# Linear attention and MLP block on one core: the last w2 chunk's raw rows loaded earlier, its split and its repeated rows moved later, the packed squares moved earlier

## The chip, the cores and the metric

The kernel runs on one core of one Trainium2 chip. The metric is the time of one execution on the device in microseconds (us); lower is better. Five engines work side by side, each through its own instructions in their written order: TensorE (PE, with its weight loads PEld), VectorE (DVE), ScalarE (ACT), GpSimd (POOL) and SyncE (SP), which here issues nearly all DMA transfers.

## The reference

```
x  : (2048, 512)          xn = layernorm(x)
A  : q, k, v = xn @ wqkv  (32 heads of 16)
     pq, pk = phi(q), phi(k);  phi(t) = (t + 1 if t > 0 else exp(t)) + 1e-6
     kv = sum over tokens of pk * v;  z = sum over tokens of pk
     o  = (pq @ kv) / (pq . z + 1e-6);   A = o @ wo
B  : h = xn @ w1 + b1     (F = 1376)
     B = relu(h)^2 @ w2 + b2
out = x + A + B
```

## The kernel before

All matrix work is in fp32 precision, made of fp32r matmuls: each operand is split into a high half (a ScalarE copy that rounds, `copy("act", h, t)`) and a low half (a VectorE subtraction, `rest_of`), and a product takes three passes: high x high, high x low, low x high (`three`, `product`).

The first part (to about 98 us in the profile) walks over 16 tiles of 128 tokens: layer norm, transpose, k projection, and the products `kx` of tokens with pk, whose column sums are also the key sum z. After it ScalarE copies the four banks of `kx` (`kxs`) and one row (`zrow`), and SyncE moves that row to DRAM (`zd`, line 878) and back as columns (`zc`, line 882, four transfers).

The second part does two rounds (n = 0, 1) of two 512-token blocks, t1 and t2. A round is a loop over passes p; each pass takes one pair of chunks of q or of w1 (`order`: q0, w0, q1, w1, ...) through a Strassen-like scheme of seven half-size products in four PSUM banks. The order of the work is written out by hand, with `manual_schedule`, so every engine runs its instructions as the lines stand. In a pass:

- A = `A11` x x1, copied by ScalarE to c11; B = `A12` x x1; VectorE adds them.
- C = `S1` x `T[1]`, copied by ScalarE to t5 (the page calls the tile t). In passes after the first, the bank `before` of the last pass is read by VectorE (line 1066) at the pass's start, and `A22` x `T[4]` is added into it after S1.
- In pass 0 of round 0, `last_sums(3, ...)` splits the token differences T[3], and `matrix()` multiplies the value sums with wo into four banks pm, which `matrix_copy(0..3)` copies to m.
- The next pass's chunk is split (`chunk_split`, tiles aop) and summed (`chunk_sums`, tiles S).
- A = `S2` x `T[2]`, copied by ScalarE to c12 (the page calls the tile c); then `S4` x x2 is added into C; VectorE adds C and c12 (line 1175). `last_sums(4, ...)` splits T[4].
- A = `S3` x `T[3]`, into the bank that c12 was copied from.

Hidden units go into the output through w2. w2 chunks are loaded raw (`piece_2`) and split into `w2r`; the closures that split wait in `w2next` and are run by `next_2` and `high_2`. The last chunk (f = NF - 1) has only 96 rows, 64 + 32. It is loaded in three pieces (line 207). Its `high()` rounds it, sends 64 rows by DMA to the low tile (line 211), and sends 32 rows four times to `w2q` (line 215); its `low()` does two VectorE subtractions. The hidden units of that chunk are packed the same way: `last_units` squares them (line 961), copies them to `sz` and sends 64 rows by DMA (`hidden_last`, line 465); `sz_rests` and `packed` subtract later. `last_2` uses sz and the last w2 chunk in pass 1, in the PSUM banks that pm had; `quarters_2` uses w2q after the loop.

Raw rows, w1 and q chunks and the sums S share six buffers ("raw"); a new one is loaded when an older one has had its last reader. wvl, a row of wqkv that is subtracted from wv in the first part (line 683), is one of them.

Of the kernel before, what the change touches and what calls it, by code (L numbers as in the profile page):

```python
# [8 lines left out]
F32R = mybir.dt.float32r  # L9
# [9 lines left out]
def kernel(  # L19
# [40 lines left out]
    NF = -(-F // P)  # L60
# [11 lines left out]
    keep = ctx.enter_context(tc.tile_pool(name="keep", bufs=1))  # L72
# [5 lines left out]
    def bank(name, tag="ps"):  # L78
        return psum.tile([P, 512], F32, name=name, tag=tag)

    def w512(name, tag, bufs):
        return work.tile([P, 512], F32, name=name, tag=tag, bufs=bufs)
# [8 lines left out]
    def two(name):  # L91
        return keep.tile([P, 2, 512], F32, name=name, tag=next_tag("x"))

    def four(name, tag, dt=F32, pool=None):
        return (pool or work).tile([P, TB, 512], dt, name=name, tag=tag)
# [4 lines left out]
    def f32(ap):  # L100
        return ap.bitcast(F32)
# [7 lines left out]
    def copy(eng, o, i, bias=0.0):  # L109
        if eng == "act":  # L110
            nc.scalar.activation(o, i, AF.Copy, bias=bias)  # L111
        elif bias:
            ENG[eng].tensor_scalar(o, i, bias, None, op0=OP.add)
        else:
            ENG[eng].tensor_copy(o, i)
# [5 lines left out]
    def rest_of(l, src, h):  # L121
        nc.vector.tensor_tensor(out=l, in0=src, in1=f32(h), op=OP.subtract)  # L122
# [40 lines left out]
    def raw(name, src):  # L163
        t = w512(name, "raw", 6)
        nc.sync.dma_start(t[:, :src.shape[-1]], src)
        return t
# [6 lines left out]
    def units(f):  # L173


        if f < NF - 1:
            return [(0, f * P, P)]
        return [(0, f * P + Q, 2 * Q), (2 * Q, f * P, Q), (3 * Q, f * P, Q)]
# [5 lines left out]
            nc.sync.dma_start(tj[:, :, a:a + n], w1[:, o:o + n].rearrange("(j p) n -> p j n", j=NJ))  # L184
        return t

    w2r = []

    def load_o():
        o = wos[0] = four("wo", "ra")  # L190
# [6 lines left out]
    def piece_2(f, at):  # L197

        h, l = w2s[f] = [w2r[at // 2][:, at % 2 * 2 + u] for u in range(2)]
        if f < NF - 1:  # L200
            t = raw(f"r2_{f}", w2[f * P:(f + 1) * P, :])
            return [lambda: copy("act", h, t), lambda: rest_of(l, t, h)]


        t = w512(f"r2_{f}", "raw", 6)
        for a, o, n in units(f):
            nc.sync.dma_start(t[a:a + n], w2[o:o + n, :])

        def high():
            copy("act", h, t)  # L210
            nc.sync.dma_start(f32(l[2 * Q:]), f32(h[:2 * Q]))
            if "q" not in w2s:
                w2s["q"] = work.tile([P, D], F32R, name="w2q", tag="w2q")
                for k in range(TB):
                    nc.sync.dma_start(f32(w2s["q"][k * Q:(k + 1) * Q]), f32(h[2 * Q:3 * Q]))

        def low():
            rest_of(l[:2 * Q], t[:2 * Q], h[:2 * Q])
            rest_of(h[3 * Q:], t[3 * Q:], h[3 * Q:])

        return [high, low]
# [230 lines left out]
    def quarters(name, r, h, pool, tag):  # L452

        lq = pool.tile([P, P], F32R, name=f"{name}q", tag=tag)
        for k in range(TB):
            at, to = slice(2 * Q, 3 * Q), slice(k * P, (k + 1) * P)
            rest_of(lq[k * Q:(k + 1) * Q], r[at, to], h[at, to])
        return lq

    def hidden_last(name, r):  # L460

        s = pair(name)
        h, hl = s[:, 0], s[:, 1]
        copy("act", h, r)
        nc.sync.dma_start(f32(hl[:2 * Q]), f32(h[:2 * Q]))

        def rests():
            rest_of(hl[2 * Q:], r[:2 * Q], h[:2 * Q])

        return (h, hl), rests  # L470

    def relu(o, i, f):
        nc.scalar.activation(o, i, AF.Relu, bias=b1s[:, f:f + 1])

    def plain_1(ps, w, x):

        for j in range(NJ):
            three(ps, [w[:, u, j * P:(j + 1) * P] for u in range(2)],
                  [x[u][:, j, :] for u in range(2)], j == 0, j == NJ - 1)
# [63 lines left out]
    for i0 in range(0, NT, TB):  # L543
# [5 lines left out]
        n = TB if i0 >= NPE else TB // 2  # L549
# [105 lines left out]
    def tokens_sum(n, tag):  # L655
        return keep.tile([P, 2, 2, 512], F32R, name=f"T{n}", tag=tag)
# [51 lines left out]
    def load_1(kind, n):  # L708
        load = raw_1 if kind == "w" else raw_q
        return [load(2 * n + k).rearrange("p (c n) -> p c n", c=2) for k in range(2)]  # L710
# [25 lines left out]
    def do(what, k=1):  # L736
        for _ in range(k):
            if what:
                what.pop(0)()
# [41 lines left out]
    def more(i=None):  # L781

        if i is None or i > 12:
            do(extra, counts[0].pop(0))
# [77 lines left out]
        more(i)  # L862

    T.update({n: tokens_sum(n, f"A{n - 3}") for n in (3, 4)})
    xlast = [xsb[(b + 1) % 2] for b in (NB - 1, NB - 2)]
    more()
    pz = bank("pz0")
# [47 lines left out]
    def matrix_copy(j, ps):  # L915
        if j % 2 == 0:
            mraw.append(two(f"m{j}"))
        copy("act", mraw[j // 2][:, j % 2], ps[j])
# [5 lines left out]


    last = TB - 1
    w2r = [four(f"w2r{k}", f"C{k}", F32R, keep) for k in range(2)]
    for n in range(2):
        t1, t2 = NB - 1 - 2 * n, NB - 2 - 2 * n
        x1, x2 = xsb  # L930
# [29 lines left out]
        def last_units(rz):  # L960
            nc.scalar.activation(rz, rz, AF.Square)
            sz, rests = hidden_last(f"sz{n}", rz)

            def packed():
                lqs.append(quarters(f"sz{n}", rz, sz[0], work, "heads"))

            return sz, rests, packed
# [3 lines left out]
        if n == 0:  # L971

            more()
            pz2 = bank("pz0b")
            plain_1(pz2, z, x2)
            more()

            rz = r2[1]
            relu(rz, pz, NF - 1)
            relu(r2[NF - 1], pz2, NF - 1)  # L980
            do(extra, 2)
            values()
            do(extra, len(extra))
            w2next = piece_2(NF - 1, 0)
        else:
            w2next = []
            pz = bank(f"pz{n}", "acc")
            plain_1(pz, z, x1)
# [4 lines left out]
        if n:  # L993
            rz = w512(f"rz{n}", "p", 6)
            relu(rz, pz, NF - 1)
            sz, sz_rests, packed = last_units(rz)
# [5 lines left out]
        def next_2(t):  # L1002

            do(w2next, 2 - highs.pop(0))
            if t + 1 < NF and (n == 0 or t >= TB - 1):
                f = w2order[t + 1]
                w2next.extend(piece_2(f, place(f)))

        def high_2():
            do(w2next)  # L1010
            highs[0] = 1
# [36 lines left out]
        def step(k=1):  # L1048

            for _ in range(k):  # L1050
                do(steps[t1] or steps[t2])

        for p in range(NO + 1):
            at_p = AT[p]
            kind, k = order[p] if p < NO else ("", 0)
            fa, fb = 2 * k, 2 * k + 1

            was, k = order[p - 1] if p else ("", 0)
            pa, pb = 2 * k, 2 * k + 1
            A, before, B, C = banks[p % 2], banks[(p + 1) % 2], *banks[2:]  # L1060
# [17 lines left out]
            if kind:  # L1078
                c11 = w512(f"c11_{n}_{p}", "p", 6)
                copy("act", c11, A)  # L1080
                if n == 0 and p == 0:
                    next_2(0)
                product(B, A12, [x[:, 2:] for x in x1], True, True)
                if kind == "w":
                    high_2()
                nc.vector.tensor_tensor(out=c11 if kind == "w" else q[t1][:, fa], in0=B, in1=c11, op=OP.add)
                if kind == "w":
                    relu(c11, c11, fa)
                else:
                    steps[t1] += steps_of(t1, fa, parts=True)  # L1090
                step(at_p[0])
# [25 lines left out]
            if p == 0:  # L1117
                def last_sums(k, *what):
                    for f in what:
                        for j in range(2):  # L1120
                            f(k, j, o34[k - 3][:, j])

                last_sums(3, difference_high, difference_low)
            if p == 1:
                nc.vector.tensor_scalar(zc[:, 1], zc[:, 0], 1e-6, None, op0=OP.mult)
                acc = [bank(f"acc{t1}_{k}", "acc") for k in range(TB)]
# [6 lines left out]
            elif not was:  # L1133

                if n == 0:
                    pm = matrix()
# [17 lines left out]
                s12, s34 = chunk_sums(p + 1, w)  # L1154
            if p + 2 < NO:
                w = load_1(*order[p + 2])
            step(at_p[3])
            if p == NO - 1 and n:
                do(bias, 2)
# [10 lines left out]
                chunk_split(0, 1, s12)  # L1170
            step(at_p[4])
            if n == 0 and p == 0:
                matrix_copy(2, pm)
            product(C, S4, [x[:, 2:] for x in x2], False, True)
            nc.vector.tensor_tensor(out=c12 if kind == "w" else q[t2][:, fa], in0=C, in1=c12, op=OP.add)
            if kind == "w":
# [21 lines left out]
                second_sums()  # L1198
            step(at_p[6])
            if n == 0 and p == 0:  # L1200
                matrix_copy(3, pm)
                sz, sz_rests, packed = last_units(rz)
            product(A, S3, [T[3][:, u] for u in range(2)])
            if p == NO - 3 + 1 - n:
                load_res(t1)
# [26 lines left out]
        f = NF - 2  # L1232
# [36 lines left out]
        for e, f in enumerate(waiting[:-2]):  # L1269
# [14 lines left out]
            if n == 0 and 1 <= e < 5:  # L1284
                k, u = divmod(e - 1, 2)
# [68 lines left out]
```

## Time and profile before

| | |
|---|---|
| median of 3 runs | 413.15 us (412.41 to 414.46) |
| profiled execution | 413.63 us, span 411.9 us |
| PE busy | 404.0 us, 98% of the span |
| DVE, ACT, POOL busy | 302.2, 263.1, 49.7 us |
| DMA | 56.34 MB, mean 137 GB/s |
| chain that ended last | PE 89%, DMA 3%, ACT 2%, DVE 2% |

Times in a profile are microseconds from the span's start. A row of the timeline gives start, length, engine, line, operation, tile written <- tiles read, shapes and the number of merged instructions; in brackets stands the engine's idle time before it and what released it. A line is often a helper's: L111 is ScalarE's copy, L119 and L122 the subtraction that makes a low half, L130 and L485 the three-pass products, so the tile names tell the places apart. The ends of matmuls are modelled.

### The profile page before, as it was taken

The page shows a single profiled execution, that of the slowest core. Times are in us where ns is not written, and L with a number is a line of the kernel's source. Part 1 is how long each engine was busy: PE and PEld are TensorE (multiplying, and loading weights), DVE is VectorE, ACT ScalarE, POOL GpSimd, SP SyncE. Part 2 cuts the span into 40 slices and gives each one's busy share as a digit, 9 for nine tenths or more (in the row PEclk, how much of TensorE's full clock was granted, in tenths as well). Part 3 has the DMA queues.
Part 4 walks back from the last instruction along what each step waited for, and adds up shares of the span by engine and source line. Part 5 has one row for each costly group of instructions (what it writes and reads, how often), then busy time and mean ns, then how long its engine had stood idle before and what let it go on. Part 6 is the DMA issues. An engine that isn't in the chain of part 4 may idle for free.

```text
span 411.9 us, 5624 instructions
## 1 busy us (share of the span) xinstructions
PE 404.0 (98%) x1947; PEld 331.2 (80%) x1947; DVE 302.2 (73%) x550; ACT 263.1 (64%) x460; POOL 49.7 (12%) x83
## 2 busy tenths in 40 slices
PE   7999999999989999999999999999999999999996
PEld 6788888888678888888878888888888888878885
DVE  5885666587699898988449967567989686449833
ACT  4666667556687779788638631577587857737520
POOL 5442333220000000030000200000000200000200
PEclk9999999999999999999999999999999999999999
DMA  6949676800442221273357992411121881024612
GB/s 207 347 142 340 193 306 205 256 1 0 104 134 72 78 75 54 77 203 53 136 221 246 362 235 90 128 53 51 51 78 29 235 183 40 2 101 154 103 26 102
DMA packets 46462, 56.34 MB, mean 137 GB/s; under 512 B 8225, under 2 KB 29985, under 8 KB 45154
## 3 DMA queue, kind: packets, MB, share of 16 engines
q1 hardware_dynamic: 44130, 51.80, 38.9%
q0 software_dynamic: 2304, 4.20, 6.2%
q8 instruction: 15, 0.25, 0.2%
q14 instruction: 13, 0.11, 0.1%
HBM read 41.43 MB, written 13.37 MB: 133 GB/s over the span
## 4 chain that ended last, share of the span: by engine, by line
PE 89%; DMA 3%; ACT 2%; DVE 2%; issue 1%; SPq 1%; POOL 0%; ACTq 0%
PE acc L130 37%; PE b L485 29%; PE kx L386 10%; PE pk L366 9%; PE acc L496 2%; DMA x<-in_A_x_dram 1%; PE pz L130 1%; DMA r<-in_B_w_dram 1%; PE b L130 1%; DMA sz<-sz 1%; ACT T L111 0%; SPq L522 0%; ACT aop L111 0%; ACT kxs L111 0%; DVE aop L119 0%
## 5 line engine op out<-in xcount | busy, mean ns | idle before, releaser
L130 PE MATMUL acc<-w2r,s 128*128 128x512 f32 x477 | 112.8, 390 | 0.0
L130 PEld LDWEIGHTS acc<-w2r,s 128*128 128x128 f32 x477 | 89.4, 188 | 19.2 <-issue 0.7
L485 PE MATMUL b<-T,aop 128*128 128x512 f32 x336 | 83.6, 390 | 1.4 <-ACT c L111 1.4
L485 PEld LDWEIGHTS b<-T,aop 128*128 128x128 f32 x336 | 62.9, 188 | 15.6 <-ACT c L111 1.8
L1034 POOL DMA_DIRECT2D res<-in_B_b_dram x16 | 14.4, 1114 | 280.2 <-DVE S L718 88.7
L386 PE MATMUL kx<-pk,tok 128*128 128x512 f32 x192 | 46.6, 391 | 0.1
L386 PEld LDWEIGHTS kx<-pk,tok 128*128 128x128 f32 x192 | 35.8, 188 | 7.9 <-ACT pk L111 0.5
L485 PE MATMUL b<-xs0h,aop 128*128 128x512 f32 x112 | 36.9, 390 | 0.0
L130 PE MATMUL acc<-mh,aTsr 128*128 128x512 f32 x112 | 35.6, 389 | 0.0
L1042 DVE TENSOR_TENSOR res<-acc,res 128x512 f32<-128x512 f32 x16 | 11.0, 692 | 21.9 <-PE acc L130 19.1
L122 DVE TENSOR_TENSOR w2r<-r,w2r 128x512 fp32r<-128x512 f32 (+2 forms) x35 | 23.8, 683 | 3.6 <-ACT w2r L111 3.5
L119 POOL TENSOR_TENSOR tok<-xp,tok 128x512 fp32r<-128x512 f32 x16 | 21.1, 1320 | 43.2 <-ACT tok L111 43.2
L130 PEld LDWEIGHTS acc<-mh,aTsr 128*128 128x128 f32 x112 | 21.0, 188 | 4.4
L485 PEld LDWEIGHTS b<-xs0h,aop 128*128 128x128 f32 x112 | 21.0, 188 | 4.4
L111 ACT ACTIVATE aop<-S 128x512 fp32r<-128x512 f32 x28 | 17.5, 626 | 10.0 <-DVE S L718 10.0
L111 ACT ACTIVATE w2r<-r 128x512 fp32r<-128x512 f32 x32 | 19.7, 620 | 6.5 <-DMA r<-in_B_w_dram 4.4
L119 DVE TENSOR_TENSOR aop<-S,aop 128x512 fp32r<-128x512 f32 x28 | 19.3, 688 | 4.8 <-ACT aop L111 4.4
L119 DVE TENSOR_TENSOR s<-c,s 128x512 fp32r<-128x512 f32 x20 | 13.5, 689 | 11.5 <-ACT s L111 11.5
L485 PE MATMUL b<-xs0l,aop 128*128 128x512 f32 x56 | 21.8, 389 | 0.0
L130 PE MATMUL acc<-ml,aTsr 128*128 128x512 f32 x56 | 21.8, 389 | 0.0
L485 PE MATMUL b<-xs1h,aop 128*128 128x512 f32 x56 | 19.6, 391 | 0.4 <-ACT t L111 0.4
L111 ACT ACTIVATE T<-Tf 128x512 fp32r<-128x512 f32 x16 | 9.5, 625 | 16.1 <-DVE Tf L661 15.9
(188 smaller groups left out, 740.9 us busy)
## 6 DMA issues: line engine op xcount, KB each, us to landing
r<-in_B_w_dram SPq DMA_DIRECT2D x49, 256.0 KB, 3.1
res<-in_A_x_dram SPq DMA_DIRECT2D x8, 512.0 KB, 4.3
res<-in_B_b_dram POOLq DMA_DIRECT2D x16, 256.0 KB, 6.0
out_dram<-res SPq DMA_DIRECT2D x15, 256.0 KB, 2.1
via<-xp SPq DMA_DIRECT2D x5, 512.0 KB, 3.0
xg<-via SPq DMA_DIRECT2D x20, 128.0 KB, 2.6
xTd<-t SPq DMA_DIRECT2D x8, 256.0 KB, 4.2
x<-in_A_x_dram SPq DMA_DIRECT2D x4, 512.0 KB, 6.1
```

The lines of the kernel that those rows point to most:

```text
L111: nc.scalar.activation(o, i, AF.Copy, bias=bias)
L119: ENG[el].tensor_tensor(out=l, in0=src, in1=f32(h), op=OP.subtract)
L122: nc.vector.tensor_tensor(out=l, in0=src, in1=f32(h), op=OP.subtract)
L130: nc.tensor.matmul(ps, lhsT=a[u], rhs=b[v], start=first and n == 0, stop=last and n == 2)
L366: nc.tensor.matmul(ps, lhsT=cols(i)[u][:, j, slot(i)], rhs=w[v][:, j, :], start=first and n == 0, stop=last and n == len(steps) - 1)
L386: nc.tensor.matmul(kxp[c], lhsT=tok[i][:, u, c * P:(c + 1) * P], rhs=pk[i][:, v], start=i == 0 and (u, v) == first, stop=i == NT - 1 and ( ...
L485: nc.tensor.matmul(ps, lhsT=a[u][:, j * P:(j + 1) * P], rhs=b[v][:, j, :], start=first and j == 0 and n == 0, stop=last and j == 1 and n == 2,
L496: nc.tensor.matmul(ps, lhsT=s[u][:, k * P:(k + 1) * P], rhs=w2s[NF - 1][u][:, a:z], start=first and u == 0, stop=stop and u == 1)
L1034: nc.gpsimd.dma_start(r[:, i], b2[None, :].partition_broadcast(P), accum_op=OP.add)
L1042: nc.vector.tensor_tensor(out=r[:, a:z], in0=ps, in1=r[:, a:z], op=OP.add)
```

## The change

- The tiles `w2r` and the loads of the last w2 chunk (`piece_2(NF - 1, 0)`) come right after the token loop, before the key sum's transfers; they came after the first values and before the chunk loop.
- `next_2(0)` of round 0, which runs that chunk's `high` and `low` and loads the next w2 chunk, comes after S1's copy and the split of T[3]; it came after the copy of A.
- The four transfers to `w2q` leave `high`; they are kept in `fourfold` and run in pass 1, after that pass's chunk loads.
- `last_units(rz)` comes between S2 and S4 of pass 0, where `matrix_copy(2)` was, and `matrix_copy(2)` goes to where `last_units` was, between S4 and S3.

```diff
-    w2r = []
+    w2r, fourfold = [], []
...
             nc.sync.dma_start(f32(l[2 * Q:]), f32(h[:2 * Q]))
             if "q" not in w2s:
                 w2s["q"] = work.tile([P, D], F32R, name="w2q", tag="w2q")
+                fourfold.append(lambda: four_times(h))
+
+        def four_times(h):
                 for k in range(TB):
                     nc.sync.dma_start(f32(w2s["q"][k * Q:(k + 1) * Q]), f32(h[2 * Q:3 * Q]))
...
     T.update({n: tokens_sum(n, f"A{n - 3}") for n in (3, 4)})
+    w2r.extend(four(f"w2r{k}", f"C{k}", F32R, keep) for k in range(2))
+    w2next = piece_2(NF - 1, 0)
     xlast = [xsb[(b + 1) % 2] for b in (NB - 1, NB - 2)]
...
     last = TB - 1
-    w2r = [four(f"w2r{k}", f"C{k}", F32R, keep) for k in range(2)]
     for n in range(2):
...
             do(extra, len(extra))
-            w2next = piece_2(NF - 1, 0)
         else:
...
                 copy("act", c11, A)
-                if n == 0 and p == 0:
-                    next_2(0)
                 product(B, A12, [x[:, 2:] for x in x1], True, True)
...
                 last_sums(3, difference_high, difference_low)
+                if n == 0:
+                    next_2(0)
...
                 w = load_1(*order[p + 2])
+            if p == 1:
+                do(fourfold)
             step(at_p[3])
...
             if n == 0 and p == 0:
-                matrix_copy(2, pm)
+                sz, sz_rests, packed = last_units(rz)
             product(C, S4, [x[:, 2:] for x in x2], False, True)
...
             if n == 0 and p == 0:
+                matrix_copy(2, pm)
                 matrix_copy(3, pm)
-                sz, sz_rests, packed = last_units(rz)
             product(A, S3, [T[3][:, u] for u in range(2)])
```

## Prediction

> **What bounds the kernel now.** I read the page first, then the list of what TensorE waited for, then the timeline of each engine from 96 to 126 us, where the changed lines run.
>
> ```profile
> span 411.9 us, 5624 instructions
> PE 404.0 (98%) x1947; PEld 331.2 (80%) x1947; DVE 302.2 (73%) x550; ACT 263.1 (64%) x460; POOL 49.7 (12%) x83
> ```
>
> TensorE has something in flight for 404.0 of 411.9 us, so only its pauses can be won. The six waits it has in the whole span are these:
>
> ```profile
> PE b L485 <- ACT c L111: 1.4, 1, 1.4
> PE pt L305 <- DVE xp L265: 1.1, 1, 1.1
> PE warm L516 <- PEq L1340: 0.8, 1, 0.8
> PE pk L366 <- DVE wkh L115: 0.4, 1, 0.4
> PE b L485 <- ACT t L111: 0.4, 1, 0.4
> PE acc L496 <- DMA sz<-sz: 0.3, 1, 0.3
> ```
>
> Three belong to the start of the kernel (lines 305, 516, 366), which the change does not touch. The other three, on lines 485 and 496, all fall in the first two passes of the chunk loop (n = 0, p = 0 and 1). The timeline shows them and their neighbours; each row has its start, its length, engine, line, operation, count, and in brackets the idle time before it and what ended that.
>
> ```profile
> 106.56 1.52 PE L485 MATMUL b<-T,aop 128*128 128x512 f32 x6
> 109.08 1.65 PE L485 MATMUL b<-T,aop 128*128 128x512 f32 x6
> 111.10 0.50 PE L485 MATMUL b<-xs1h,aop 128*128 128x512 f32 x1 [0.37 <-ACT t L111]
> 112.37 0.40 PE L485 MATMUL b<-xs1h,aop 128*128 128x512 f32 x1
> 114.12 1.64 PE L485 MATMUL b<-T,aop 128*128 128x512 f32 x6 [1.36 <-ACT c L111]
> 118.32 2.88 PE L485 MATMUL b<-T,aop 128*128 128x512 f32 x12
> 121.04 0.39 PE L496 MATMUL acc<-w2r,sz 128*128 128x512 f32 x1
> 121.73 1.85 PE L496 MATMUL acc<-w2r,sz 128*128 128x512 f32 x7 [0.30 <-DMA sz<-sz]
> 123.42 1.52 PE L485 MATMUL b<-T,aop 128*128 128x512 f32 x6
> ```
>
> In pass 0 the products come in the order A11, A12, S1 (106.56), the value matrix, S2 (109.08), S4 (111.10), S3 (114.12). Now ScalarE beside them:
>
> ```profile
> 109.93 0.63 ACT L111 ACTIVATE w2r<-r 128x512 fp32r<-128x512 f32 x1 [3.87 <-DMA r<-in_B_w_dram]
> 110.47 0.58 ACT L111 ACTIVATE t<-b 128x512 f32<-128x512 f32 x1
> 110.95 1.14 ACT L111 ACTIVATE T<-Tf 128x512 fp32r<-128x512 f32 x2
> 111.99 1.07 ACT L111 ACTIVATE m<-pm 128x512 f32<-128x512 f32 x2
> 112.94 0.64 ACT L111 ACTIVATE aop<-r 128x512 fp32r<-128x512 f32 x1
> 113.46 0.60 ACT L111 ACTIVATE c<-b 128x512 f32<-128x512 f32 x1
> 124.98 0.60 ACT L111 ACTIVATE c<-b 128x512 f32<-128x512 f32 x1 [0.65 <-PE b L485]
> ```
>
> ScalarE stands 3.87 us in front of the high half of the last w2 chunk, because its raw rows have not landed. Behind it in ScalarE's own order stand the copy t of product S1, which S4 needs (it adds into the same bank), and c, which frees the bank for S3. So one late load makes both pauses of 0.37 and 1.36 us. The third wait is for rows that SyncE moves from one half of sz to the other.
>
> **What a pause costs.** Matmuls overlap: twelve without a pause take 2.88 us (118.32) and one takes 0.39, so the pace is (2.88 - 0.39) / 11 = 0.227 us. I count from start to start. S2 ends at 110.73, its last matmul started at 110.34, S4 could have followed at 110.57 and came at 111.10: 0.53 lost, and 0.12 more, since six matmuls behind a pause last 1.64 where they last 1.52 (106.56). S3 could have started at 112.37 + 0.23 = 112.60 and came at 114.12: 1.52 + 0.12. The second sz matmul could have started at 121.27 and came at 121.73: 0.46, and 0.10 more by its own row (1.85 for seven, 1.75 at the pace). Together 2.85 us, the most that can be won here. The idle column alone (0.37 + 1.36 + 0.30) makes it 2.03. The Trainium skill (Perfetto Trace Analysis, Identifying the Most-Contended Engine) warns that pipelined matmuls make the busy share a poor measure of TensorE's headroom; by the busy column the forecast below would have to stay under 2.03, and the starts quoted above are what I go by instead.
>
> **The change part by part.**
>
> *The early load.* The three loads of the raw rows (line 207) move ahead of the key sum's transfers on SyncE.
>
> ```profile
> 101.13 0.29 SPq L878 DMA_DIRECT2D zd<-zrow  x1
> 105.01 1.57 SPq L207 DMA_DIRECT2D r<-in_B_w_dram  x3
> 106.62 2.58 SPq L184 DMA_DIRECT2D r<-in_B_w_dram  x2
> 111.18 2.49 SPq L215 DMA_DIRECT2D w2q<-w2r  x4
> 96.03 0.68 DVE L683 TENSOR_TENSOR wv<-wv,wvl 128x512 f32<-128x512 f32 x1
> ```
>
> They need one of six raw buffers. Of those in use, the ones with wvl and the last w1 chunk are done first; wvl's last reader is the row on line 683, ending at 96.71. So the loads issue from 96.71 to 98.3, before SyncE has anything else to do (zd at 101.13 waits for its row anyway), and zd and zc stay where they are. The loads of the next w1 chunk (line 184) step up from 106.62 to 105.0. They were taken at 112.94 without a wait, so at most 6.3 us after their issue; even that slowest case gives 111.3, where ScalarE now wants them at 111.13 (below). Cost of this part: nothing to 0.2 us, and I take nothing. The rows now have eleven us to land in before they are read, where they had five.
>
> *The split moved two products later.* ScalarE's order becomes t, T, T, w2r, m, m, aop, c instead of w2r, t, T, T, m, m, aop, c: the same eight copies, from 109.93 to the start of c at 113.46 in 3.53 us for the first seven. It starts as soon as S1 is there. Where ScalarE waited only for a product (the c at 124.98), it began 0.43 us after the start of the last matmul (123.42 + 1.52 - 0.39 = 124.55). For S1 that is 106.56 + 1.52 - 0.39 + 0.43 = 108.12. So t ends near 108.7, well ahead of S4 at 110.57: that pause is gone (0.65). c starts at 108.12 + 3.53 = 111.65, ends at 112.25, and S3 starts at 112.31 (0.06 behind it, as at 114.12). TensorE could start it at 110.57 + 6 x 0.227 = 111.93, so a pause of 0.38 + 0.12 = 0.50 is left of 1.64: 1.14 won.
>
> *The packed squares one product sooner.* Line 961 and the copy behind it, with the transfer of line 465, come before the sums T4 and before two of the copies m. ScalarE's rows, and last the transfer as the chain that ended last has it:
>
> ```profile
> 116.44 1.14 ACT L111 ACTIVATE T<-Tf 128x512 fp32r<-128x512 f32 x2
> 117.96 0.63 ACT L961 ACTIVATE r2c<-r2c 128x512 f32<-128x512 f32 x1
> 118.62 0.64 ACT L111 ACTIVATE sz<-r2c 128x512 fp32r<-128x512 f32 x1
> 119.33 2.26 DMA sz<-sz
> ```
>
> The copy of sz at 118.62 moves by the 1.9 us by which its surroundings come sooner (VectorE, next paragraph), and by the T and m copies it passes (1.04 + 0.96): about 114.7. Its transfer then goes at 115.4 and lands at 117.7 (2.26, chain row). TensorE asks for sz at 121.04 - 1.81 = 119.23. The 0.56 of the third pause is won, with 1.5 us to spare; VectorE's own rows of sz follow at about 118.4, with 0.8. The two m copies that slip behind now end about 117.3; the bank they free is wanted from 119.2 on.
>
> *What is late next: VectorE.* It now has T's low halves, then w2r's, then the chunk's:
>
> ```profile
> 110.60 1.41 DVE L122 TENSOR_TENSOR w2r<-r,w2r 64x512 fp32r<-64x512 f32 x2 [3.52 <-ACT w2r L111]
> 113.84 0.69 DVE L119 TENSOR_TENSOR aop<-r,aop 128x512 fp32r<-128x512 f32 x1
> 117.45 1.29 DVE L122 TENSOR_TENSOR T<-Tf,T 128x512 fp32r<-128x512 f32 x2
> 118.65 0.69 DVE L1066 TENSOR_TENSOR q<-b,t 128x512 f32<-128x512 f32 x1
> ```
>
> The last T copy of ScalarE starts at 109.12 and ends at 109.73, its low half is done at 110.5; w2r's two take 1.41, so the chunk's low half starts near 111.9 instead of 113.84, 1.94 sooner. From there to line 1066 VectorE ran 4.81 us without a gap. But ScalarE now does 1.2 us of squares (117.96 to about 119.16) in place of one 0.5 us copy ahead of T4; T4 was there 0.39 us early (117.06 against 117.45), so line 1066 starts 0.3 to 0.4 later than that: 111.9 + 4.81 + 0.35 = 117.06, end 117.75. Product A22, which adds into the bank that line 1066 reads, starts 6 x 0.227 = 1.36 after the row at 118.32, at 119.68; less 1.81 that is 117.87. A margin of 0.1 us where it was 0.34: without cover here each tenth that VectorE is late is a tenth lost. I put 0 to 0.4 on this and take 0.15.
>
> *The repeated rows.* Four transfers (line 215, 2.49 us of issuing) leave SyncE's queue between line 211 and the next load and go behind the loads of pass 1. They are read only after the loop, by quarters_2. In pass 1, SyncE then stands idle in front of its next load (first row of two from SyncE's waits between 97 and 136 us):
>
> ```profile
> SPq L184 <- DVE dt L432: 4.5, 1, 4.5
> SPq L207 <- DVE aop L119: 0.4, 1, 0.4
> ```
>
> 4.5 us cover 2.49; the price is nothing, and were that cover gone the load behind would be 2.5 us later.
>
> **Sum.** 0.65 + 1.14 + 0.56 - 0.15 = 2.2 us; bounds 1.7 (0.2 for the chunk load, 0.4 for VectorE) and 2.85. The profiled execution took 413.63 us, 1.7 outside its span; it would take 411.4, span 409.7. The median of the three runs shown is 413.15, 0.5 below that execution, so I predict 411.0. That is 0.52% less, and 0.5% (2.07 us) is about what a measurement of this kernel can tell from no change.
>
> **The rivals.**
>
> *VectorE takes the place of the wait.* If T4 comes later by the full 0.7 us, or w2r's low halves push the chunk further back, TensorE waits at A22 of pass 1, and the next pass finds VectorE as far behind. For it: the margin of 0.1. Against: VectorE is busy 73%. Twice 0.4 us more leaves 1.4 won: 411.7.
>
> *The gain is given back.* All three pauses go, but a later stage waits for what does not come sooner, and the end stays: 413.1. Against it, no other wait of TensorE is in the list after 123 us; but what was hidden has no row.
>
> *Slower: the early load blocks SyncE.* Its queue is in order. If the raw buffer it gets is released not at 96.71 but by the VectorE copy that the SyncE row above names for line 207 (it ends at 105.35), then zd goes at 105.35 + 1.57 = 106.92, 5.79 later, and line 184 at 105.01 + 5.79 = 110.80. If it lands L later, S3 starts at 110.80 + L + 1.18 (aop, c, release). With L from 2.26 (the sz transfer) to 6.3 that is 114.2 to 118.3, and without any gain it would be 112.31 + 2.35 = 114.66: from 0.4 won to 3.6 lost. I take 2.0 lost: 415.1. It decides once the release is later than about 101.4 (L = 6.3) to 105.4. Against it: line 207 issued at 105.01, before that copy had ended, so the named releaser is not the real one. The Trainium skill (DMA: Bandwidth & Descriptors, Anatomy of one DMA) speaks for this rival: a DMA's semaphore wait is sat out on the issuing sequencer, ahead of dispatch. The trace agrees that SyncE can stand in a queue (4.5 us, row above).
>
> **How the numbers follow.** Forecast 0.63, VectorE 0.22, given back 0.07, blocked queue 0.08. The forecast's own range is 410.3 to 411.5; with 0.3 for the scatter of a median, the VectorE case in full and part of the unchanged case, 8 in 10 is 410.1 to 413.2. Faster by over 0.5%: 0.7 of the forecast and a small part of the VectorE case, 0.47. Slower by over 0.5%: two thirds of the blocked queue, 0.06. Within: 0.47.
>
> **What would show it.** Right: line 207 at about 97 us on SyncE, w2r on ScalarE without idle time at about 109.7, t at 108.1, a wait of TensorE for ACT c of about 0.2 to 0.3 (by the idle column), none for sz; sz copied near 114.7. Wrong: zd later than 101.2, a wait of line 485 for DVE q of more than 0.3 near 118, or a new wait of TensorE after 130 us.

## The result, and the profile after

The changed kernel takes 411.90 us (median of 22 runs, 410.95 to 413.51), the kernel before 413.07 us (22 runs, 411.22 to 415.07). The ratio is 0.9973, with a 95% interval from 0.9961 to 0.9985: faster by 1.2 us, where 2.15 us were forecast, and within 0.5%. That lies below the sum's lower bound (1.7 us), and the median is above the forecast's own range (410.3 to 411.5); only the wider range, which also holds the rivals, covers it. The profiled execution took 410.98 us, span 409.3 us.

The waits of TensorE in the whole span of the changed kernel, as the list of before:

```profile
PE warm L519 <- PEq L1345: 0.8, 1, 0.8
PE pt L308 <- DVE xp L268: 0.5, 1, 0.5
PE pk L369 <- ACT xs1h L324: 0.3, 1, 0.3
PE b L488 <- ACT c L111: 0.2, 1, 0.2
```

The waits for ACT t and for sz are gone, of the one for ACT c 0.2 us is left. The timeline of the changed kernel around the change (lines have moved by 3 to 6; rows of TensorE, ScalarE, VectorE and SyncE):

```profile
103.16 0.50 PE L488 MATMUL b<-xs0h,aop 128*128 128x512 f32 x1
111.78 1.66 PE L488 MATMUL b<-T,aop 128*128 128x512 f32 x6 [0.21 <-ACT c L111]
116.00 3.00 PE L488 MATMUL b<-T,aop 128*128 128x512 f32 x12
118.84 2.00 PE L499 MATMUL acc<-w2r,sz 128*128 128x512 f32 x8
120.67 1.52 PE L488 MATMUL b<-T,aop 128*128 128x512 f32 x6
107.60 0.60 ACT L111 ACTIVATE t<-b 128x512 f32<-128x512 f32 x1 [2.08 <-PE b L488]
109.13 0.62 ACT L111 ACTIVATE w2r<-r 128x512 fp32r<-128x512 f32 x1
111.13 0.60 ACT L111 ACTIVATE c<-b 128x512 f32<-128x512 f32 x1
114.14 0.63 ACT L111 ACTIVATE sz<-r2c 128x512 fp32r<-128x512 f32 x1
116.54 0.68 DVE L1069 TENSOR_TENSOR q<-b,t 128x512 f32<-128x512 f32 x1
88.28 1.58 SPq L207 DMA_DIRECT2D r<-in_B_w_dram  x3
100.58 0.26 SPq L883 DMA_DIRECT2D zd<-zrow  x1
125.00 2.48 SPq L218 DMA_DIRECT2D w2q<-w2r  x4
```

In this execution the chunk loop begins 0.56 us sooner than in the profile before (103.16 against 103.72): the first part has waits of its own, on lines 308 and 369, that differ from one execution to the next. So I measure one stretch, from the start of the first chunk product to the start of S2 of pass 1: 103.16 to 120.67 is 17.51 us, and before it was 103.72 to 123.42, 19.70. The profiles differ by 2.19 us here, to a hundredth what the prediction's sum says; the medians differ by 1.2. The experiments had to find the missing microsecond.

### The profile page after: what moved, and what is told of

Read it like the earlier page. It is cut to its first block, busy times and chain, and to the rows that moved or that the text cites. A ratio compares the mean times of both kernels' runs of the same rounds, so it can differ in the third digit from the quotient of the medians.

```text
span 409.3 us, 5622 instructions
## 1 busy us (share of the span) xinstructions
PE 403.9 (99%) x1947; PEld 332.1 (81%) x1947; DVE 303.3 (74%) x550; ACT 262.7 (64%) x460; POOL 49.4 (12%) x83
## 4 chain that ended last, share of the span: by engine, by line
PE 96%; ACT 1%; DMA 1%; DVE 0%; issue 0%; POOL 0%; ACTq 0%; POOLq 0%
PE acc L130 37%; PE b L488 32%; PE pk L369 11%; PE kx L389 11%; PE acc L499 2%; PE pz L130 1%; DMA x<-in_A_x_dram 1%; PE b L130 1%; PE pz0b L130 1%; PE pt L308 1%; PE acc L506 0%; PE pkv L899 0%; ACT m L111 0%; ACT T L111 0%; PE end L130 0%
## 5 line engine op out<-in xcount | busy, mean ns | idle before, releaser
L111 ACT ACTIVATE aop<-S 128x512 fp32r<-128x512 f32 x28 | 17.5, 624 | 9.5 <-DVE S L721 9.5
```

## The experiments

Two theories. **The stall**: ScalarE's order makes each microsecond that the raw rows come late a microsecond of TensorE, and what the change brings is as large as the stall happens to be. **A new cost**: the stall is always that of the first profile, and something in the changed kernel, as VectorE in pass 1 or the moved transfers, takes a microsecond back in most executions. Medians stand beside those of before on the same chip.

| kernel | stretch | ScalarE idle before w2r | median, before | ratio (95%) |
|---|---|---|---|---|
| before | 19.70 | 3.87 | | |
| before, second profile (e4) | 17.79 | 2.00 | | |
| repeats only (e8) | 18.90 | 3.10 | 413.21, 413.24 | 1.0007 (0.9985 to 1.0029) |
| squares only (e11) | 19.89 | 4.35 | 413.09, 413.16 | 0.9995 (0.9975 to 1.0016) |
| load later (e10) | 23.14 | 5.80 | 416.22, 413.16 | 1.0055 (1.0033 to 1.0078) |
| no early load (e2) | 18.03 | 0.56 | 412.51, 413.01 | 0.9979 (0.9961 to 0.9997) |
| load and split (e7) | 17.77 | 0 | 411.78, 413.24 | 0.9969 (0.9947 to 0.9990) |
| the change (first profile) | 17.51 | 0 | 411.90, 413.07 | 0.9973 (0.9961 to 0.9985) |
| the change again (e5) | 17.46 | 0 | 411.72, 413.24 | 0.9956 (0.9936 to 0.9977) |
| load between zd and zc (e9) | 17.36 | 0 | 411.98, 413.16 | 0.9961 (0.9942 to 0.9979) |
| load only (e1) | 17.16 | 0 | 410.93, 413.01 | 0.9948 (0.9929 to 0.9968) |
| load and squares (e6) | 16.88 | 0 | 411.17, 413.24 | 0.9944 (0.9919 to 0.9969) |
| the change, split first (e3) | 16.87 | 0 | 410.96, 413.01 | 0.9942 (0.9922 to 0.9962) |
| load, squares, second place (e12) | 16.87 | 0 | 410.54, 413.16 | 0.9933 (0.9910 to 0.9956) |

**e4, before again.** No edit.

> The kernel before, profiled a second time. If its stall varies with the landing of the raw rows: ScalarE's idle time in front of w2r differs from 3.87 us by half a microsecond or more, the three pauses of TensorE add up to clearly less than 2.85 us by starts, about 1.5, which would make the medians' gain of 1.2 the usual one. If it does not vary: 3.8 to 3.9 us and 2.8 to 2.9 again, and the missing microsecond is lost in the changed kernel or in the first part.

ScalarE in front of w2r in this second profile, and TensorE at sz and at S2 of pass 1:

```profile
108.85 0.63 ACT L111 ACTIVATE w2r<-r 128x512 fp32r<-128x512 f32 x1 [2.00 <-DMA r<-in_B_w_dram]
104.50 0.50 PE L485 MATMUL b<-xs0h,aop 128*128 128x512 f32 x1
120.62 1.83 PE L496 MATMUL acc<-w2r,sz 128*128 128x512 f32 x7 [0.24 <-DMA sz<-sz]
122.29 1.52 PE L485 MATMUL b<-T,aop 128*128 128x512 f32 x6
```

2.00 us of idle time where the first profile had 3.87, and a stretch of 17.79 where it had 19.70. The time at which the rows land is not the same from one execution to the next, and between 2 and 3.9 us of idle time the stretch follows it one to one: less the idle time it is 15.8 in both, and in e8 too (18.90 - 3.10). Below that it can't: about the first 1.6 us are free (an estimate), since with the rows there early ScalarE stands 1.56 us in front of t for S1 (e1 below). Of these three profiles of before's order, the first had the slowest load; e11 below has a slower one.

**e8, repeats only.**

```diff
+                fourfold.append(lambda: four_times(h))
...
+            if p == 1:
+                do(fourfold)
```

> Before with only the repeated rows moved. They are on no path: ratio 1.000, within 0.3%; ScalarE's idle time in front of w2r between 2 and 4 us as in the two profiles of before. If their 2.5 us of SyncE's queue held up loads that TensorE or VectorE needs: 0.3 to 1 us faster.

Ratio 1.0007: the repeated rows cost nothing that can be told in either place. As a third look at before's order it has 3.10 us of idle time.

**e1, load only.**

```diff
+    w2r.extend(four(f"w2r{k}", f"C{k}", F32R, keep) for k in range(2))
+    w2next = piece_2(NF - 1, 0)
     xlast = ...
```

> The kernel before with the early load of the raw rows as its only edit. If the late load is the cause: ScalarE no longer stands before w2r, c ends near 111.7 us, S3 starts without a pause, the pause for sz stays at about 0.6 (TensorE is there sooner, sz is not): 2.1 us off the span, nearly all that the whole change brought in its profile (2.2 between the first product and S2 of pass 1). If the split's place is the cause: nothing off, since w2r still stands ahead of t. If the profile of before caught an unusually slow load: 2.1 in the profile, but only about 1 us between the medians, as with the whole change (413.07 to 411.9).

One edit brings at least what all four bring together: 0.9948 (the interval overlaps the change's), a stretch of 17.16 where the change has 17.5, and no wait of TensorE in the second part at all. Rows of ScalarE and TensorE:

```profile
105.39 0.62 ACT L111 ACTIVATE w2r<-r 128x512 fp32r<-128x512 f32 x1
107.57 0.60 ACT L111 ACTIVATE t<-b 128x512 f32<-128x512 f32 x1 [1.56 <-PE b L485]
111.39 1.53 PE L485 MATMUL b<-T,aop 128*128 128x512 f32 x6
118.20 2.26 PE L496 MATMUL acc<-w2r,sz 128*128 128x512 f32 x8
120.30 1.52 PE L485 MATMUL b<-T,aop 128*128 128x512 f32 x6
```

S3 (111.39) has no pause. Of the 0.6 us that I expected to stay at sz about half stays, although the list has no wait: the eight sz products take 2.10 us from start to start (118.20 to 120.30), where e6 below has 1.81 (118.13 to 119.94). So the other half of the squares' wait was the stall's own consequence.

**e3, split first**: the change with `next_2(0)` back behind the copy of A.

```diff
                 copy("act", c11, A)
+                if n == 0 and p == 0:
+                    next_2(0)
```

> The changed kernel with the split of the last w2 chunk back ahead of t. With the rows there early, ScalarE copies w2r at about 105.5 us while it waits for S1 anyway; c ends 0.5 us sooner, S3 starts without a pause, VectorE has w2r's low halves done 4 us sooner and reaches the chunk's low half sooner. Theory: 0.4 to 0.6 us better than the change (medians near 411.4). Rival, that VectorE's line 1066 is the bound in pass 1: no better than the change (411.9).

Stretch 16.87, and 410.96. The same with the repeats at their old place is **e6, load and squares**, run beside the change itself, **e5**:

> Before with the early load and the earlier squares; split and repeated rows at their old places. If the repeated rows cost nothing wherever they stand: a stretch of 16.9 us and a median near 410.9, as with the repeats moved. If their place matters (2.5 us of SyncE's queue ahead of the next chunk's loads): a new wait of ScalarE for a load, a stretch of 17.2 or more.

> The changed kernel once more, on one chip with its parts. Stretch from the first chunk product to S2 of pass 1 (called the stretch): 17.5 us in its first profile, 17.2 with the early load alone, 16.9 with load, squares and repeats but the split at its old place. If only the pause that is left before S3 and the rest of the stretch tell them apart, this stretch is 17.4 to 17.6 again and the median lies 0.3 to 0.7 us above the load alone (near 411.5). If the changed kernel has a wait that its first profile missed: a stretch over 17.8, or more than 285 us behind it.

ScalarE in e6, and TensorE at S3, at S1 and A22 of pass 1, at sz and at S2. Here w2r fills time in which ScalarE would wait for S1 anyway:

```profile
105.31 0.62 ACT L111 ACTIVATE w2r<-r 128x512 fp32r<-128x512 f32 x1
107.47 0.60 ACT L111 ACTIVATE t<-b 128x512 f32<-128x512 f32 x1 [1.54 <-PE b L485]
110.48 0.61 ACT L111 ACTIVATE c<-b 128x512 f32<-128x512 f32 x1
111.30 1.53 PE L485 MATMUL b<-T,aop 128*128 128x512 f32 x6
115.39 2.90 PE L485 MATMUL b<-T,aop 128*128 128x512 f32 x12
118.13 1.98 PE L496 MATMUL acc<-w2r,sz 128*128 128x512 f32 x8
119.94 1.52 PE L485 MATMUL b<-T,aop 128*128 128x512 f32 x6
```

t comes 2.16 us after w2r, and 1.54 us of them ScalarE still stands idle; c is 3.01 us behind t, where in the change it is 3.53 (107.60, 111.13). The changed kernel's stretch is 17.46 again: 0.58 us behind e6 in the stretch, 0.55 between the medians of that chip (411.72, 411.17; the intervals of the two overlap). Most of it is the pause that the prediction left at S3 (0.50). The rest is at A22 of pass 1: S1 and A22 take 2.84 us from start to start in the change (116.00 to 118.84) and 2.74 in e6 (115.39 to 118.13). Behind the stretch, e5 has what the change's first profile did not have: a wait of 0.3 us for VectorE's s near 249 us, with 285.20 us from S2 of pass 1 to the start of TensorE's last row instead of 284.67. The kernel before has that wait too (e4); e12 returns to it.

**e7, load and split**: squares and repeats at their old places, `next_2(0)` late.

> Before with the early load and the split moved later; squares and repeats at their old places. If the later split costs what the copies ahead of c cost: a pause of about 0.2 (idle) before S3 as in the changed kernel, and the wait for sz comes back with 0.1 to 0.3; stretch 17.6 to 17.9, median 0.4 to 0.8 above the load alone. If the split's place is free: 17.2 as with the load alone.

The pause at S3 and one of 0.19 at sz are both in the list, stretch 17.77. The earlier squares thus are worth 0.3 us (17.77 - 17.46), and 0.3 as well with the split first (17.16 - 16.88). Alone they bring nothing that can be told (**e11**): the wait for sz goes, but S1 and A22 of pass 1 now take 2.94 us from start to start where before has 2.72, so nearly half of what sz gives comes back there; and the stall stays, here with 4.35 us of idle time.

> Before with the packed squares one product sooner as its only edit. If the wait for sz is a cost of its own: TensorE no longer waits for DMA sz, 0.4 to 0.6 us off the stretch (18.2 to 18.5 where before has 18.8 on the mean of three profiles), ratio 0.9985 to 0.9990, while the wait for ScalarE's c stays. If it only shows because the stall ahead has put everything late: the wait turns into one for VectorE at A22 and the ratio is 1.000.

**e2, no early load**: the change with `piece_2(NF - 1, 0)` back behind zc.

> The changed kernel with the load of the raw rows back at its old place behind zc. If order is enough: w2r comes up in ScalarE's order at about 109.6 us, the rows land near 109.9 as before, ScalarE stands 0.3 us, c ends at about 112.3 to 112.6, the gain is that of the whole change less 0 to 0.3 us (medians near 412.0). If the early load is what counts: the stall of some 3 us moves behind T, c comes 2 us later, and the time is that of before (413.1).

Order alone covers most of the flight: ScalarE stands 0.56 us, TensorE 0.88 in front of S3.

```profile
114.50 1.66 PE L488 MATMUL b<-T,aop 128*128 128x512 f32 x6 [0.88 <-ACT c L111]
```

18.03 is about 0.55 worse than the change (17.51, 17.46). The ratio (0.9979) is clear of 1, but not of the change's, nor of that of the squares alone (e11), which e2 has as well; that order by itself gains is read from the rows.

**e9, load between zd and zc.**

```diff
     nc.sync.dma_start(zd, zrow[P - 1:])
+    w2r.extend(four(f"w2r{k}", f"C{k}", F32R, keep) for k in range(2))
+    w2next = piece_2(NF - 1, 0)
```

> Before with the raw rows' load between zd and zc, the only edit. In three profiles with the load behind zc its rows landed 8.8, 6.9 and 8.0 us after zd's issue. If the wait behind zc's four transfers is what makes it late: it issues 0.4 us after zd (while zc would stand for zd's landing anyway), lands by 105 us, no idle time in front of w2r, stretch 17.2 us and a median of 410.9 to 411.2, as with the load ahead of everything. If the rows' own flight is slow whenever zd and zc are under way: idle time of 0.5 us or more stays, stretch 17.5 or more.

No idle time in front of w2r, and a stretch of 17.36 (forecast 17.2): being ahead of zc is enough. The median was forecast 0.8 to 1.1 us lower; in the profile TensorE lost 1.38 us at another place, shown under e12. That this explains the median was not tried.

**e10, load later**: `piece_2(NF - 1, 0)` behind `load_1(*order[1])`.

> Before with the load one place later, behind the two loads of the next w1 chunk (line 184), the only edit. If each microsecond that the rows come later goes through ScalarE's order into the time: 1.0 to 2.6 us later (their issue), stretch 19.5 to 21, median 414.0 to 415.5. If the wait is covered elsewhere: 413.1.

The dose in the other direction: 5.80 us of idle time, 3.1 us slower, and above the forecast of 414.0 to 415.5. In this profile the stretch is 1.5 us longer than 15.8 + 5.80, and the granted clock fell to a half for part of it. The columns are from and to, length, busy time of TensorE, its weight loads, VectorE, ScalarE and GpSimd, granted clock, busy share of the DMA engines, GB/s:

```profile
95.00:113.00 18.00, 15.71 (x218) 11.71 (x217) 10.05 (x17) 9.10 (x18) 0.00 (x0) 1.00 0.18 46
113.50:120.20 6.70, 6.14 (x15) 4.36 (x14) 6.63 (x14) 5.66 (x12) 0.00 (x0) 0.50 0.69 174
120.50:130.00 9.50, 9.50 (x43) 7.82 (x42) 7.97 (x18) 6.62 (x13) 0.00 (x0) 1.00 0.27 70
```

The profiled execution has a mean clock of 0.992 over its span, and one other of the twelve has 0.996; the other ten have 0.999 or more, so the median's 3.1 us do not come from such a fall.

**e12, the same cure at a second place.** In most profiles TensorE waits for nothing after 123 us; in e2, e4, e5, e7, e9 and e11 it waits 0.2 to 1.4 us for VectorE's s between 249 and 252 us. Behind it is the same pattern in e9: ScalarE stands for the last w1 chunk's raw rows, and the copy s stands behind it.

```profile
242.91 0.63 ACT L111 ACTIVATE w1z<-r 128x512 fp32r<-128x512 f32 x1 [4.83 <-DMA r<-in_B_w_dram]
243.45 0.62 ACT L111 ACTIVATE s<-r2c 128x512 fp32r<-128x512 f32 x1
249.65 0.49 PE L130 MATMUL acc<-w2r,s 128*128 128x512 f32 x1 [1.38 <-DVE s L119]
```

```diff
-                if e == 7:
-                    zs()
...
                 if k == 0:
+                    zs()
                     prepare = operands_first(1, w)
```

> Before with the early load, the earlier squares, and the same cure at a second place near 240 us: the split of the last w1 chunk (zs) stands behind the first of the last two hidden splits instead of ahead of it. In twelve profiles ScalarE stood 2.2 to 4.8 us there for that chunk's rows, and where it was 3.6 or more TensorE waited up to 1.4 us for VectorE's s near 249. If that is the same in-order stall: no wait of TensorE for DVE s, 284.6 to 284.9 us from S2 of pass 1 to the end, a stretch of 16.9, and a median near 410.8, at or a little below load and squares alone (411.17). If w1z is then late for its own product at 255 us: a wait of line 130 there, and no gain or a loss.

ScalarE's rows with the split behind s:

```profile
238.13 0.62 ACT L111 ACTIVATE s<-r2c 128x512 fp32r<-128x512 f32 x1
240.75 0.63 ACT L111 ACTIVATE w1z<-r 128x512 fp32r<-128x512 f32 x1 [2.01 <-DMA r<-in_B_w_dram]
```

s no longer stands behind that load, and no wait of TensorE is listed outside the first part. But this load was quick: in the old order ScalarE would have stood about 2.6 us (from 238.13 to 240.75), and the profiles with up to 3.56 us there have no wait for s anyway. So the rows show the new order, not a wait that it took away. 410.54, ratio 0.9933, is the lowest median of all and below both kernels; its interval is clear of the change's (0.9961 to 0.9985), but overlaps those of e5 and e6. What the second place is worth stays open.

## Why the prediction was right, and where its size was wrong

- **ScalarE's order as the cause of both pauses in pass 0: right.** e1 takes the late load away and both are gone; e10 makes it later, and the two together grow from 1.73 to 2.85 us (idle column: 0.37 and 1.36 before, 2.29 and 0.56 in e10). An earlier place of the load (e9) or the later place of the split (e2) takes most of ScalarE's idle time away by itself: 0 and 0.56 us are left.
- **The times of the changed pass: right.** With the 0.56 us of the earlier start taken off, c was forecast to start at 111.09 (it started at 111.13), S3 at 111.75 (111.78), the copy of sz at 114.1 (114.14), line 1066 at 116.5 (116.54), and S2 of pass 1 at 120.66 (120.67).
- **The step that failed: "What a pause costs", 2.85 us.** The term was right for that execution and wrong as a typical one. Against 16.88 without pauses, before's order lost 2.82, 0.91 and 2.02 us in three profiles (19.70, 17.79, 18.90), 1.9 on average; the change loses 0.6 (17.51, 17.46). The difference is 1.3, near the medians' 1.2 and 1.5. The sum used one flight of a DMA as if it were a constant. A hint was in the table of times: the profiled execution was itself 0.5 us above the median, and I carried the whole gain over to the median. That this is the whole of the missing microsecond is not shown. e11 has the load at before's place too and stood 4.35 us; counted in by its idle time (15.8 + 4.35), the average loss is 2.3 and the difference 1.7 (an estimate). And the stretch is not all that varies: in e4 it was 1.91 us shorter than in the first profile of before, but the chunk loop began 0.78 us later and the part behind the stretch took 0.67 us more, so the span was only 0.4 us shorter.
- **The sum in its own execution: right, term by term.** By starts, the pause of S4 went (0.65), S3 kept 0.51 of its 1.64, sz lost 0.02 instead of 0.56, and A22 lost 0.12: 0.65 + 1.13 + 0.54 - 0.12 = 2.20, and the stretches differ by 2.19. That is more than the idle column's 2.03. The starts were the better measure; the medians can't tell the two apart.
- **VectorE takes the place of the wait: by a tenth of a microsecond, as set aside.** Line 1066 (1069 in the changed kernel) ends at 117.22, and A22 could have started at 116.00 + 6 x 0.227 = 117.36: the margin was 0.1, as worked out. But it did not cover: S1 and A22 take 2.84 and 2.83 us from start to start in the change's two profiles, and 2.72 before (118.32 to 121.04). No wait is listed for it; the row at 116.00 is 3.00 long where before has 2.88. The prediction left no time between the end of line 1066 and the start of the product. In e6, where the same margin was 0.26 us, the two products take 2.74, and little was lost. Of the 0.15 us set aside, 0.12 were needed.
- **The blocked queue: did not happen, but my reason for that was off.** The loads waited for the buffer of the last w1 chunk (its split by VectorE), not for wvl's, and issued at 88.28, eight microseconds before the 96.71 I gave. zd stood at 100.58, 0.55 ahead of before, as everything else in that execution.
- **The repeats at nothing: right** (e8, to within its interval), and the 4.5 us of SyncE's idle time held them: 125.00 to 127.48 with the next load of that line after 129.
- **Not seen in advance: the late split costs.** The prediction called the 0.50 us left at S3 a remainder. With the load early it is the price of moving the split: e6 and e3 do not have it. Of the change's four parts, the load brings 2.1 us against before (e1, medians), the squares 0.3 in the stretch on top, the repeats nothing, and the later split takes back about 0.6 in the stretch where the load is early, while by the rows it gains where the load is late (e2). By times the change, e1, e3 and e6 are not told apart: their intervals overlap.

## What to carry to other kernels

A stall of an in-order engine behind a load is worth what the load's flight happens to be, less what the engine would have waited anyway, and that differs from one execution to the next; size it from two or three profiles, or say how far the one profile stands from the median, before carrying a gain over. Two cures for one stall do not add: issue the load early, and then put the copy into the time in which its engine waits anyway, ahead of the copies that another engine needs. When a stall is cured, look for the same pattern elsewhere; here the second place had a wait in six of the fourteen profiles and none in the others.

## What the runs showed of the hardware

- The same transfer, from the same place in the order, ended ScalarE's idle time after 2.00 (e4), 3.10 (e8), 3.87 (before) and 4.35 us (e11). The four tiny zc transfers ahead of it took 1.77 us to issue in e4 and 2.61 in the first profile; what sets this was not tried.
- In e10 TensorE's granted clock fell to 0.50 from about 113.4 to 120.3 us, after a pause of 2.29 us (idle column; 2.68 from the start of the last product to the start of the next) in front of S4. It fell about 0.6 us after TensorE had started again (112.87). The Trainium skill (TensorE: Matmul & The Clock Gate, Part 1: The HAM clock gate) gives the half clock after an idle window of about 3.4 us. The pause here was shorter than that, so for this execution the measurement decides; the 6.8 us at half clock are about two such windows (an estimate). In this execution the stall was thus paid for a second time. In the other profiles, with pauses up to 1.36 us, the clock in this stretch stayed at 1.00. It is one execution; where between 1.36 and 2.29 us the clock begins to fall was not tried.
